# Two VectorE passes instead of three for each converted weight, range checks moved into the MLPs, and a new written-out order

## The chip, the core and the metric

The kernel runs on one core of one Trainium2 chip. The metric is the device time of one execution in microseconds; the median of three executions of the kernel before is 641.96 us (640.41 to 643.04).

## The reference, cut to what matters

A linear recurrence runs over 768 steps for 4 x 8 heads of dimension 40, and its output goes through an MLP without a nonlinearity other than one product:

```python
for t in range(S):                                  # S = 768
    y[:, :, t] = einsum('bhd,bhde->bhe', r_t, state)
    Sa = einsum('bhde,bhe->bhd', state, a_t)
    state = state * w_t[:, :, None, :] - einsum('bhd,bhe->bhde', Sa, b_t)
    state = state + einsum('bhd,bhe->bhde', v_t, k_t)
x = y.transpose(0, 2, 1, 3).reshape(3072, 320)
h = ((x @ w1) * (x @ w2)) @ w3                      # w1, w2: 320 x 1024, w3: 1024 x 1024
out = (h @ w_out).astype(float32)                   # w_out: 1024 x 320
```

The weights arrive as 64-bit floats. The kernel reads them as 64-bit integers and makes 32-bit floats of them on the chip.

## The kernel before, in words

The 768 steps are cut into 12 chunks of 64 (`NCH`), and the 32 heads into two groups (`NG`). For a chunk and group the kernel loads a block `fm` (decays and two operands) and a block `lh` through SyncE's queue (`load`), makes running products of the decays on VectorE and scales the operands with them on VectorE or GpSimd (`scale`, L397 to L422), and forms the products inside a chunk on TensorE (`causal`, L446). For a chunk, `solve` inverts the triangular matrices that couple its steps: a transpose into PSUM (tile `ab`, L478), some 40 short VectorE operations (L504 to L527) and two transposes (L554, L557), the results of which stand in `TDX`. For the first three chunks `merge` (L582 to L594) does a part of this on TensorE, between a first and a second L557. `join` (L618, L625) builds the joined inverse in `TT`, with four ScalarE copies `TT<-TDX` at its end. `pairs` (L662) and `tokens` (L689) prepare operands. `rec` is the recurrence proper: for a group TensorE does L713, L720, L728 and L744 one after the other, with ScalarE copies and GpSimd masks between them, and L779 carries the state on; it depends on the chunk before. `gather` (L801) moves the chunk's output `y` into the MLP's layout `xr` by twelve DMAs, and `mlp` does the MLP of a chunk: 128 matrix products with `W12` (L843) and 48 with `W3` (L869), 16 and 7 us of TensorE.

`W3` stands for w3 @ w_out, which is multiplied out once (`product`, L365). An MLP needs `W12`, that is w1 and w2, in a high and a low part: a ScalarE copy makes the high part and a GpSimd subtraction (L343, L355) the low one.

`weights` and `convert` make the 32-bit weights, in 16 pieces of up to 128 x 1024 (15.5 pieces' worth, 1 MB each): a DMA into `raw` (two buffers), on ScalarE a square (L291) and an exponential (L294), each with a sum that serves a range check, and on VectorE three passes: L297 with one input, L301 and L304 with two. The order of pieces is: one row block of w1 and w2, then w_out, then w3 with the products, then the rest of w1 and w2. The sums are judged at the very end of the program text (L1016 to L1027), in instructions that do not belong to the written-out order: the judging of the weights' sums (L1019) was put where its inputs were ready, between two passes of the last piece. The verdict decides whether a slow general path runs; in these executions it does not.

Nothing is scheduled at run time. Each engine runs its instructions in the order in which they were written, and `PLAN`, a packed table of numbers, sets that order for all of them (`Order.place`), together with the buffer that each tile takes. `SLOTS` says how many buffers a tile has.

Of the kernel before, what the change touches and what calls it, by code (L numbers as in the profile page):

```python
# [1096 lines left out]
```

## Time and profile before

| | before |
|---|---|
| median of 3 executions | 641.96 us |
| the profiled execution | 644.88 us |
| its span, first to last instruction | 643.2 us |
| mean granted TensorE clock | 0.974 |
| TensorE (PE) busy | 575.1 us, 89% |
| VectorE (DVE) busy | 464.4 us, 72% |
| ScalarE (ACT) busy | 465.6 us, 72% |
| GpSimd (POOL) busy | 243.7 us, 38% |
| DMA moved | 57.65 MB, 90 GB/s |

Busy times are summed over each engine's instructions; a share says nothing yet on where an engine waits. The span is 1.68 us shorter than the execution's own time, and that execution was 2.92 us longer than the median.

### The profile page before, as it was taken

To read this page: it belongs to the slowest core of one execution; us is meant where nothing else is said; L and a number is where in the kernel's file an instruction comes from. 1 tells how busy PE (TensorE), PEld (TensorE's weight loads), DVE (VectorE), ACT (ScalarE), POOL (GpSimd) and SP (SyncE) were. 2 spreads that over 40 slices of the span, in tenths; PEclk is the share of its full clock that TensorE was granted. 3 is DMA by queue.
4 is the path that set the end of the run, shared out by engine and by line. 5 is a ranking of instruction groups with operands and counts; after the bars stand their busy time and mean duration, and the time that the engine had idled before them with its cause. 6 is when DMAs were issued, how large, how long until landed. Compare 5 with 4: busy or idle time off the path is not lost.

```text
span 643.2 us, 23611 instructions
## 1 busy us (share of the span) xinstructions
PE 575.1 (89%) x10226; PEld 521.6 (81%) x10226; DVE 464.4 (72%) x795; ACT 465.6 (72%) x962; POOL 243.7 (38%) x229
## 2 busy tenths in 40 slices
PE   0534989969999999899999999999999999999996
PEld 0424666649899999899999989998898999999995
DVE  7997989795469789369789695897796875931320
ACT  1785778888866977777977878778777689676321
POOL 5152075143551315542426336236254165321011
PEclk9999998976999999899999999999998999999998
DMA  8755466433314314314243144143340341211101
GB/s 191 220 142 200 147 217 170 121 94 89 73 33 93 87 43 93 83 48 107 59 98 93 37 99 85 46 99 78 82 112 20 88 110 33 63 26 29 32 21 25
DMA packets 58935, 57.65 MB, mean 90 GB/s; under 512 B 29320, under 2 KB 52360, under 8 KB 56904
## 3 DMA queue, kind: packets, MB, share of 16 engines
q1 hardware_dynamic: 58824, 56.07, 34.4%
q8 instruction: 82, 1.34, 0.9%
q14 instruction: 29, 0.24, 0.1%
HBM read 47.40 MB, written 3.93 MB: 80 GB/s over the span
## 4 chain that ended last, share of the span: by engine, by line
PE 62%; DVE 16%; DMA 9%; ACT 6%; issue 4%; POOL 1%; SPq 1%; DVEq 0%; POOLq 0%; ACTq 0%
PE bank L843 21%; PE bank L869 12%; DMA fm<-in_fmx_dram 6%; PE bank L365 4%; PE bank L720 4%; PE bank L744 4%; PE bank L446 3%; PE bank L728 2%; PE bank L713 2%; DVE tmp L504 2%; PE bank L689 2%; PE bank L779 2%; PE bank L618 2%; PE bank L625 2%; DVE mf L301 2%
## 5 line engine op out<-in xcount | busy, mean ns | idle before, releaser
L843 PE MATMUL bank<-xs,W 128*128 128x256 f32 x1536 | 204.9, 286 | 1.6 <-issue 1.5
L843 PEld LDWEIGHTS bank<-xs,W 128*128 128x128 f32 x1536 | 187.7, 189 | 8.1 <-issue 2.0
L177 ACT ACTIVATE xu<-bank 64x416 f32<-64x416 f32 (+2 forms) x280 | 123.8, 462 | 34.8 <-PE bank L728 16.6
L737 POOL TENSOR_SCALAR_AFFINE_SELECT xu<-xu 64x512 f32<-64x512 f32 x48 | 37.1, 773 | 152.8 <-ACT xu L177 136.2
L860 POOL TENSOR_TENSOR gl<-ga,gh 128x512 fp32r<-128x512 f32 x32 | 44.2, 1384 | 74.6 <-ACT gh L177 74.5
L177 ACT ACTIVATE JP<-bank 32x512 f32<-32x512 f32 (+1 forms) x120 | 59.8, 500 | 17.3 <-PE bank L446 9.8
L857 DVE TENSOR_TENSOR ga<-bank,ga 128x512 f32<-128x512 f32 x48 | 32.7, 684 | 49.9 <-PE bank L843 20.7
L464 POOL TENSOR_SCALAR_AFFINE_SELECT lh<-lh 64x512 f32<-64x512 f32 x48 | 38.6, 808 | 66.4 <-ACT lh L177 65.0
L869 PE MATMUL bank<-W3h,gh 128*128 128x320 f32 x192 | 63.7, 332 | 0.0
L869 PE MATMUL bank<-W3l,gh 128*128 128x320 f32 x192 | 60.5, 315 | 0.0
L869 PE MATMUL bank<-W3h,gl 128*128 128x320 f32 x192 | 60.5, 315 | 0.0
L672 POOL TENSOR_SCALAR_AFFINE_SELECT xu<-xu 64x512 f32<-64x512 f32 x48 | 39.6, 828 | 27.2 <-ACT xu L177 25.4
L177 ACT ACTIVATE gh<-ga 128x512 fp32r<-128x512 f32 x48 | 30.0, 628 | 22.7 <-DVE ga L857 22.0
L177 ACT ACTIVATE ga<-bank 128x512 f32<-128x512 f32 x48 | 28.5, 594 | 24.1 <-PE bank L843 21.5
L744 PE MATMUL bank<-xu,bk 128*40 128x104 f32 (+1 forms) x768 | 41.1, 260 | 5.4 <-POOL xu L737 5.3
L720 PE MATMUL bank<-xu,lh 104*64 104x104 f32 (+2 forms) x768 | 44.1, 267 | 1.9 <-ACT xu L177 0.9
L422 POOL TENSOR_TENSOR fm<-fm,gi 104x1024 f32<-104x1024 f32 x12 | 31.3, 2611 | 38.1 <-DMA rv<-in_rv_dram 13.7
L397 DVE TENSOR_TENSOR_SCAN fm<-fm,first 104x520 f32<-104x520 f32 x24 | 31.6, 1317 | 17.8 <-DMA fm<-in_fmx_dram 17.7
L409 POOL TENSOR_TENSOR lh<-lh,fm 104x1024 f32<-104x1024 f32 x16 | 35.3, 2208 | 21.5 <-DVE fm L397 18.8
L720 PEld LDWEIGHTS bank<-xu,lh 104*64 104x64 f32 (+2 forms) x768 | 38.0, 144 | 6.5 <-issue 1.9
L744 PEld LDWEIGHTS bank<-xu,bk 128*40 128x40 f32 (+1 forms) x768 | 35.4, 121 | 9.5 <-POOL xu L737 7.2
L478 DVE STREAM_TRANSPOSE ab<-JP 128x1024 f32<-128x1024 f32 x12 | 24.0, 2004 | 26.0 <-ACT JP L177 26.0
(104 smaller groups left out, 1189.9 us busy)
## 6 DMA issues: line engine op xcount, KB each, us to landing
fm<-in_fmx_dram SPq DMA_DIRECT2D x24, 627.2 KB
raw<-in_w3t_dram SPq DMA_DIRECT2D x8, 1024.0 KB
rv<-in_rv_dram SPq DMA_DIRECT2D x48, 160.0 KB
raw<-in_w_dram SPq DMA_DIRECT2D x4, 1024.0 KB
lh<-in_fma_dram SPq DMA_DIRECT2D x48, 80.0 KB
xu<-in_vt_dram SPq DMA_DIRECT2D x48, 80.0 KB
out_dram<-o SPq DMA_DIRECT2D x48, 80.0 KB
xr<-y SPq DMA_DIRECT2D x72, 40.0 KB
```

The source lines that it names most:

```text
L177: act.activation(out_, in_, AF.Copy, scale=scale)
L397: dve.tensor_tensor_scan(out=w, data0=w, data1=first.rearrange("p n t -> p (n t)"), initial=0.0, op0=ALU.mult, op1=ALU.max)
L409: e.tensor_tensor(out=lh.t[0:104], in0=lh.t[0:104], in1=gam(c, g)[:, :, 0:C].unsqueeze(1).to_broadcast(full), op=ALU.mult)
L464: pool.affine_select(out=lh.t[q, ab], in_=lh.t[q, ab], pattern=[[0, NP], [1, C]], compare_op=ALU.is_gt, fill=0.0, base=0, channel_multipli ...
L672: op("pool", 0.67, due + 2, lambda q=q, ab=ab: pool.affine_select(out=xu.t[q, ab, :, 0:C], in_=xu.t[q, ab, :, 0:C], pattern=[[0, NP], [1, ...
L720: pe.matmul(out=view(hp[h])[64 * ab:64 * ab + 64, u], lhsT=lh.t[k, ab, HP * h + u], rhs=xu.t[k, ab, HP * h + u], start=True, stop=True)
L737: pool.affine_select(out=u, in_=u, pattern=[[0, NP], [1, C]], compare_op=ALU.is_gt, fill=0.0, base=0, channel_multiplier=-1)
L744: pe.matmul(out=q(r, p), lhsT=bk.t[:, p, r], rhs=xu.t[:, ab, p], start=(c == 0), stop=True, skip_group_check=True)
L843: pe.matmul(out=pt.t[:, TOK * x:TOK * x + TOK], lhsT=WT[k][:, cs], rhs=xs.t[:, z], start=(n == 0), stop=(n == 7))
L857: op("dve", 0.69, t, lambda a=a, pt=pt: dve.tensor_tensor(out=a.t, in0=wide(pt), in1=a.t, op=ALU.mult), r=[pt], w=[a])
L860: both(ON["gl"][c % NCH], 1.3, 0.69, t + 1, lambda e, a=a, j=j: e.tensor_tensor(out=gl.t[:, j:j + 2], in0=a.t, in1=gh.t[:, j:j + 2], op=AL ...
L869: pe.matmul(out=pt.t[:, 0:DM], lhsT=l.t[:, j, ts], rhs=W3[r][:, j], start=(j == 0 and n == 0), stop=(j == NJ - 1 and n == 2))
```

## The change

A piece of weights is now converted in two VectorE passes of two inputs each. What the third pass did (bringing in bits of the low word) is prepared by one ScalarE copy of 16-bit numbers into a new tile `low`, which has one buffer. `raw` has three buffers instead of two. Pieces of w1 and w2 are converted in halves of 512 columns (`KW`), and so are their ScalarE copies and GpSimd subtractions. w_out and w3 come first now, and all of w1 and w2 after them.

The range checks no longer use what `convert` has loaded. 31 pieces of 512 columns are read from memory anew, from the first MLP on, into a tile `ck` with one buffer: a DMA of 512 KB, a ScalarE square with a sum, and a VectorE minimum. Their judging is now part of the written-out order (`verdict`), before the program's end.

`solve` writes the transposed inverse straight into the right half of `TT`, which has two buffers now, so that `join` copies two blocks instead of four. `fm` and `lh` have five buffers instead of four. The table `PLAN` is new: the work is ordered anew throughout.

```diff
-SLOTS = dict(rc=1, fm=4, lh=4, ..., JP=2, TT=1, bank=6, raw=2, sq=1, mf=2, w3f=2, ...)
+SLOTS = dict(rc=1, fm=5, lh=5, ..., JP=2, TT=2, bank=6, raw=3, ck=1, low=1, mf=2, w3f=2, ...)
 PLAN = """
-c-oa%3Ak0ok*?}<?%PywnGiBAnM{@u1H>ebVTeKy1F|bf6crRSfFL^>hA1fN7!}zBmDL!7h!6o~Q4usIG11THr_LBM!OR$u;7o#ovOL~9UGrCU-*eA>IL<
+c-nPX378edwLVqdmzfb<kQhZ-1R;DVE`(K)C4d_yfDi;R(SQatfk2{091t842%;i_AjngORb>~WL=gcIf}?_9Kt)7@s2@-LU}Tx)R-N~ss_wph!8iAtzJ0
...
-ON = dict(ws="p", ...)
+ON = dict(ws="ppppp", ...)
 def convert(src, dst, due, w=(), n=CW):
-    raw, sq, mf = slot("raw"), slot("sq"), slot("mf")
+    raw, low = slot("raw"), slot("low")
+    sources.extend(src[:, f:min(f + KW, n)] for f in range(0, n, KW))
+    parts = [slot("mf") for _ in range(0, n, KW)] if dst is None else [None]
     def f2():
-        act.activation(sq.t[:, 0:n], raw.t.bitcast(BF16)[:, 3:4 * n:4], AF.Square, accum_out=wstats[:, k:k + 1])
+        act.activation(low.t.bitcast(U16)[:, 0:2 * n:2], raw.t.bitcast(U16)[:, 1:4 * n:4], AF.Copy, scale=7.49 / 65535.0)
-    def f3():
-        act.activation(sq.t[:, 0:n], sq.t[:, 0:n], AF.Exp, scale=-2.0 ** 23, accum_out=wstats[:, NCV + k:NCV + k + 1])
-    def f4():
-        dve.tensor_scalar(out=M(), in0=H(), scalar1=3, scalar2=0xC0000001, op0=ALU.logical_shift_left, op1=ALU.bitwise_or)
-    def f5():
-        dve.scalar_tensor_tensor(out=M(), in0=H(), scalar=0x3FFFFFFF, in1=M(), op0=ALU.bitwise_or, op1=ALU.bitwise_and)
-    def f6():
-        dve.scalar_tensor_tensor(out=M() if dst is None else dst().bitcast(U32), in0=L(), scalar=29, in1=M(), ...)
+    def f3(i, M):
+        dve.scalar_tensor_tensor(out=M(), in0=H(a, b), scalar=3, in1=low.t[:, a:b], op0=ALU.logical_shift_left, op1=ALU.bitwise_or)
+    def f4(i, M):
+        dve.scalar_tensor_tensor(out=M(), in0=H(a, b), scalar=0x3FFFFFFF, in1=M(), op0=ALU.bitwise_or, op1=ALU.bitwise_and)
+def ranges(k, due):
+    raw, n = slot("ck"), sources[k].shape[-1]
+    B = lambda: raw.t.bitcast(BF16)[:, 3:4 * n:4]
+    def f1():
+        sp.dma_start(out=raw.t[:, 0:n], in_=sources[k])
+    def f2():
+        act.activation(B(), B(), AF.Square, accum_out=wstats[:, k:k + 1])
+    def f3():
+        dve.tensor_reduce(out=wstats[:, NCV + k:NCV + k + 1], in_=B(), axis=mybir.AxisListType.X, op=ALU.min)
+    op("sp", 0.351, due - 8, f1, r=["W12"], w=[raw, "turn"], dma=5.0 * n / 1024)
...
 def solve(c, due, span):
-        TD = tdx.t[:, 0:512].rearrange("x (p t) -> x p t", t=32)
+        TD = tt.t[:, :, 32:64]
-        dve.transpose(out=tdx.t[:, 512:1024], in_=tdx.t[:, 0:512])
+        dve.transpose(out=tdx.t.rearrange("x (p t) -> x p t", t=32), in_=tt.t[:, :, 32:64])
 def join(c, due):
-    for q in range(4):
-        op("act", 0.65, due + 5, lambda r=r, q=q: copy(tt.t[r, :, 32 * (q % 2):32 * (q % 2) + 32], half(0)[r]), ...)
+    for b in range(2):
+        op("act", 0.65, due + 2, lambda r=r: copy(tt.t[r, :, 0:32], tt.t[r, :, 32:64]), r=[(tt, "e", b)], w=[(tt, "c", b)])
```

**VectorE at the first chunk's merge.** Of the kernel before, from the first chunk's transpose to the sum that ends its merge (L594); TensorE's merge products stand between the two. A name's number tells one tile from the next; `w3f` and `wof` are converted weights.

```order
L557 STREAM_TRANSPOSE TDX_99<-TDX_99 128x512
L304 SCALAR_TENSOR_TENSOR wof<-raw_138,mf_141 128x512
L297 TENSOR_SCALAR mf_141<-raw_139 128x1024
L301 SCALAR_TENSOR_TENSOR mf_141<-raw_139,mf_141 128x1024
L304 SCALAR_TENSOR_TENSOR w3f_147<-raw_139,mf_141 128x1024
L594 TENSOR_TENSOR TDX_99<-bank_132,TDX_99 128x16x16
```

Of the change, the same stretch, whose transpose stands two rows above (L298 and L302 are the two passes, L412 to L433 belong to `scale`, L612 is the sum that was L594):

```order
L302 SCALAR_TENSOR_TENSOR w3f_155<-raw_144,w3f_155 128x1024
L412 SCALAR_TENSOR_TENSOR fm_93<-fm_93,first 104x520
L493 STREAM_TRANSPOSE ab<-JP_113 128x1024
L519 TENSOR_TENSOR tmp<-DG,ab 128x4
L523 TENSOR_REDUCE DG<-tmp 128x4
L519 TENSOR_TENSOR tmp<-DG,ab 128x16
L298 SCALAR_TENSOR_TENSOR w3f_154<-raw_145,low_146 128x1024
L302 SCALAR_TENSOR_TENSOR w3f_154<-raw_145,w3f_154 128x1024
L428 SCALAR_TENSOR_TENSOR gt_100,stats<-fm_93,gi_99 104x512
L433 SCALAR_TENSOR_TENSOR gi_99<-gt_100,gi_99 104x512
L523 TENSOR_REDUCE DG<-tmp 128x4x2
L612 TENSOR_TENSOR TT_114<-bank_136,TT_114 128x16x16
```

Before, four operations stand between the transpose and the sum; now twelve do, four passes and the next chunk's transpose (L493) among them.

**VectorE at the last piece of w1 and w2.** Of the kernel before (L772 is the state of `rec`):

```order
L297 TENSOR_SCALAR mf_141<-raw_139 128x1024
L301 SCALAR_TENSOR_TENSOR mf_141<-raw_139,mf_141 128x1024
L1019 TENSOR_SCALAR stats<-stats 128x16
L304 SCALAR_TENSOR_TENSOR mf_141<-raw_139,mf_141 128x1024
L772 TENSOR_TENSOR st_107<-bank_129,fm_92 104x160
```

Of the change:

```order
L519 TENSOR_TENSOR tmp<-DG,ab 128x144
L298 SCALAR_TENSOR_TENSOR mf_147<-raw_143,low_146 128x512
L302 SCALAR_TENSOR_TENSOR mf_147<-raw_143,mf_147 128x512
L298 SCALAR_TENSOR_TENSOR mf_148<-raw_143,low_146 128x512
L302 SCALAR_TENSOR_TENSOR mf_148<-raw_143,mf_148 128x512
L523 TENSOR_REDUCE DG<-tmp 128x4x6
```

The judging (L1019) is gone from this place, and the last piece runs in two halves.

**TensorE ahead of the first MLP.** Of the kernel before, the rows that stand 20 to 16 rows ahead of the first product of an MLP (L843); L582 and L588 are the third chunk's merge, L720 and L728 the second group's recurrence of the second chunk:

```order
L582 MATMUL bank_129<-TDX_99,JP_110 32x16 x64
L720 MATMUL bank_134<-xu_102,lh_95 64x104 x8
L720 MATMUL bank_132<-xu_102,lh_95 64x104 x8
L588 MATMUL bank_129<-TDX_99,wa 32x16 x64
L728 MATMUL bank_132<-hs_106,TT_112 64x104
```

Of the change, the second five of the first MLP's rows (L857, which was L843), and what follows them, the second group's recurrence (L734, which was L720):

```order
L857 MATMUL bank_135<-xs_1539,W_0_86 128x256 x2
L857 MATMUL bank_135<-xs_1539,W_2_87 128x256
L857 MATMUL bank_135<-xs_1539,W_1_1356 128x256 x2
L857 MATMUL bank_135<-xs_1539,W_3_1357 128x256
L857 MATMUL bank_135<-xs_1539,W_4_1358 128x256 x2
L734 MATMUL bank_136<-xu_105,lh_98 64x104 x8
L734 MATMUL bank_138<-xu_105,lh_98 64x104 x8
```

The third chunk's merge and the second group's L720 and L728 now stand behind the first MLP's first products instead of ahead of them.

## Rows read from the trace of the kernel before

**Rows 1.** Busy time by stretch: length, PE, PEld, DVE, ACT, POOL, PEclk, DMA share, GB/s.

```profile
17.00:64.00 47.00, 21.99 (x601) 18.62 (x601) 41.60 (x60) 35.07 (x74) 15.76 (x12) 1.00 0.64 185
64.00:143.10 79.10, 70.00 (x1175) 51.43 (x1175) 69.07 (x110) 63.41 (x123) 31.83 (x22) 0.93 0.51 154
143.10:157.20 14.10, 12.97 (x401) 11.58 (x401) 8.06 (x16) 11.27 (x24) 4.75 (x2) 0.57 0.29 73
157.20:636.60 479.40, 469.97 (x8054) 439.81 (x8050) 332.65 (x598) 352.66 (x736) 182.15 (x172) 0.99 0.29 67
```

**Rows 2.** Timeline of TensorE ahead of the first MLP: start, length, engine, what.

```profile
156.32 0.94 PE L728 MATMUL bank<-hs,TT 64*64 64x104 f32 x32
157.19 2.99 PE L843 MATMUL bank<-xs,W 128*128 128x256 f32 x23
```

**Rows 3.** Timeline of VectorE from the last piece to the first MLP.

```profile
139.47 2.55 DVE L1019 TENSOR_SCALAR stats<-stats 128x16 f32<-128x16 f32 x1 [0.36 <-ACT sq L291]
141.93 1.21 DVE L304 SCALAR_TENSOR_TENSOR mf<-raw,mf 128x1024 uint32<-128x1024 uint32 x1
...
150.50 1.91 DVE L397 TENSOR_TENSOR_SCAN fm<-fm,first 104x520 f32<-104x520 f32 x1 [2.85 <-DMA fm<-in_fmx_dram]
153.17 0.96 DVE L829 TENSOR_TENSOR xs<-xr,xs 128x768 fp32r<-128x768 f32 x1 [0.77 <-ACT xs L826]
```

**Rows 4.** Instructions that read `raw`: duration ns minimum/median/maximum, first and last start.

```profile
L297 DVE TENSOR_SCALAR mf<-raw x16: 419/686/1345, 24.1 to 136.8; 128x1024 uint32<-128x1024 uint32 x15, 128x512 uint32<-128x512 uint32 x1
L301 DVE SCALAR_TENSOR_TENSOR mf<-raw,mf x16: 668/1224/3269, 25.8 to 137.5; 128x1024 uint32<-128x1024 uint32 x15, 128x512 uint32<-128x512 uint32 x1
```

**Rows 5.** Groups by line and shape: busy us, mean ns, idle before and its releasers.

```profile
L297 DVE TENSOR_SCALAR mf<-raw 128x1024 uint32<-128x1024 uint32 x15 | 11.8, 789 | 2.3 <-DMA raw<-in_w3t_dram 1.6 <-POOL W L343 0.6
L294 ACT ACTIVATE sq<-sq 128x1024 f32<-128x1024 f32 x15 | 15.8, 1053 | 0.3
```

**Rows 6.** Timeline of VectorE's memsets at the start.

```profile
5.39 0.91 DVE L225 MEMSET SB<- 104x1024 f32 x1 [0.16 <-issue]
```

**Rows 7.** What VectorE waited for from 7 to 157.2 us: total, times, longest.

```profile
DVE TDX L594 <- PE bank L588: 7.4, 3, 3.9
DVE fm L397 <- DMA fm<-in_fmx_dram: 3.4, 2, 2.9
...
DVE mf L297 <- DMA raw<-in_w3t_dram: 1.6, 1, 1.6
```

**Rows 8.** Timeline of VectorE and GpSimd near 30 us.

```profile
30.00 3.27 DVE L301 SCALAR_TENSOR_TENSOR mf<-raw,mf 128x1024 uint32<-128x1024 uint32 x1
29.44 2.75 POOL L422 TENSOR_TENSOR fm<-fm,gi 104x1024 f32<-104x1024 f32 x1 [13.68 <-DMA rv<-in_rv_dram]
```

**Rows 9.** Timeline of TensorE between 116 and 186 us.

```profile
116.16 0.72 PE L588 MATMUL bank<-TDX,wa 32*32 32x16 f32 x64
117.90 0.73 PE L588 MATMUL bank<-TDX,wa 32*32 32x16 f32 x64
177.79 1.65 PE L720 MATMUL bank<-xu,lh 128*64 128x104 f32 x32
184.83 0.94 PE L728 MATMUL bank<-hs,TT 64*64 64x104 f32 x32
```

**Rows 10.** Groups by line and shape, of work that is nearest to the new.

```profile
L291 ACT ACTIVATE sq<-raw 128x512 f32<-128x512 bf16 x1 | 0.7, 666 | 0.0
L291 ACT ACTIVATION_READ_ACCUMULATOR sq<-raw 128x1 f32 x16 | 3.1, 194 | 0.0
L508 DVE TENSOR_REDUCE Tp<-tmp 128x64 f32<-128x512 f32 x18 | 12.3, 683 | 0.4
L177 ACT ACTIVATE TT<-TDX 32x512 f32<-32x512 f32 x48 | 30.1, 627 | 2.9 <-DVE TDX L594 1.9 <-DVE TDX L554 0.2
```

**Rows 11.** What SyncE's queue waited for in the whole execution, its longest.

```profile
SPq L385 <- DVE y L791: 59.2, 9, 10.3
```

More of the change, by code (lines that the diff above doesn't have):

```diff
@@ new lines, in convert @@
+        op("sp", 0.35, due - 8, f1, w=[raw, "turn"], dma=5.0 * n / CW)
+        op("act", 0.21 + 0.852 * n / CW, due, f2, r=[raw], w=[low])
+        for i, mf in enumerate(parts):
+            M = (lambda mf=mf: mf.t) if mf else lambda: dst().bitcast(U32)
+            to = [mf] if mf else w
+            op("dve", 0.17 + 1.071 * step / CW, due, lambda i=i, M=M: f3(i, M), r=[raw, low], w=to, two=True)
+            op("dve", 0.17 + 1.071 * step / CW, due, lambda i=i, M=M: f4(i, M), r=[raw, "conv"], w=to, two=True)
@@ L330, in weights @@
+        for ib in range(NJ):
+            w3f = slot("w3f")
+            convert(w3t[ib], lambda w3f=w3f: w3f.t, due, w=[w3f])
+            due += step
+            product(ib, w3f, due)
+        op("nil", 0.0, due, second, w=["reg2"])
+        for k in range(3):
             for f in range(2048 // CW if k < 2 else DFF // CW):
-                cs = slice(CW * f, CW * f + CW)
-                due = split(k, f, cs, due)
-                due += step
-        op("nil", 0.0, due, third, r=[("W", k, f) for k in range(3) for f in range(2)], w=["W12", "conv"])
+                due = split(k, f, slice(CW * f, CW * f + CW), due) + step
@@ L336, in split @@
+        op("nil", 0.0, due, third, r=[("W", k, f, i) for k in range(3) for f in range(2) for i in range(2)], w=["W12", "conv"])
     def split(k, f, cs, due):
         over = ["conv"] if k == 0 else ["conv", "reg2"]
-        if k < 2:
-            mf = convert(w12[k * 128:k * 128 + 128, cs], None, due)
-            def f2(e):
-                e.tensor_tensor(out=WT[2 + k][:, cs], in0=mf.t.bitcast(F32), in1=WT[k][:, cs], op=ALU.subtract)
-            op("act", 1.06, due, lambda: copy(WT[k][:, cs], mf.t.bitcast(F32)), r=[mf, *over], w=[("W", k, f)])
-            both(ON["ws"], 2.45, 1.22, due, f2, r=[mf, *over], w=[("W", k, f)])
-            return due
@@ L348, in split @@
[L348 to L356 removed]
+        parts = convert(w12[k * 128:k * 128 + 128, cs] if k < 2 else w12c[:, cs], None, due)
@@ L629, in blocks @@
             return t[r].rearrange("x (p t) -> x p t", t=32)
[L631 to L632 removed]
+        op("pe", 1.1, due, f1, r=[tdx, *[(jp, g, 2 * i) for g in range(NG) for i in range(2)]], w=[p1], kind="32")
         for b in range(2):
```

255 lines of the change are left out of this document (130 added, 125 removed).

## The prediction

> **What bounds the kernel now.** I first cut the span into stretches, because the shares of the whole (PE 89%, DVE and ACT 72%) mix two quite different stages [rows 1]. From 157.2 us, where the first MLP's products begin, to the last product TensorE is busy 469.97 of 479.40 us at a granted clock of 0.99: there TensorE is the bound, and all that can be had is the 9.4 us in which it idles. Ahead of it the picture is the reverse. From 17 to 64 us TensorE is busy 22 of 47 us, from 64 to 143 us 70 of 79 us with part of it at a lower clock (mean 0.93), and from 143 to 157 us the granted clock is 0.57, near the lower of its two levels, 1.2 GHz. VectorE in the same stretches is busy 41.6 of 47 and 69.1 of 79 us. So the kernel has a first stage of 157 us that VectorE sets, and a second that TensorE sets. TensorE's work after the first MLP's start is the same whatever happens before. So the question is when the first MLP starts, and how much of TensorE's work is left then.
>
> Second, what holds that start: the timeline of VectorE ahead of it [rows 3]. The last pass over the last piece (L304) starts at 141.93 us, behind the judging L1019, which waits 0.36 us and takes 2.55 us for 16 columns. Then VectorE waits 2.85 us for a load of `fm`, and makes the MLP's low input (L829) from 153.17 to 154.13 us. TensorE takes the MLP up at 157.19 us, as it is still in the work that stands ahead in its order [rows 2].
>
> **The change part by part, as a sum for the MLP's start.**
>
> Conversion: a piece of 1024 columns costs medians of 0.69 us for the one-input pass and 1.22 us for each two-input pass, a half 0.67 us [rows 4]. Before: 15.5 pieces x (0.69 + 1.22 + 1.22) = 48.5 us. After: 10.5 pieces of w_out and w3 x 2 x 1.22 = 25.6 us, and 5 pieces of w1 and w2 x 4 halves' passes x 0.67 = 13.4 us, together 39.0 us. Term: -9.5 us; at most -12.2 us, if the removed passes are taken as they ran (11.8 us for 15, [rows 5], and 0.42 us for the half).
>
> These rows show that the removed pass was the cheapest: it ran at almost twice the others' rate. The Trainium skill states why (VectorE: DVE Perf Modes, section "Mode 2×_2P — use both read ports for one tensor"): an operation with one tensor input may use both read ports, one with two inputs can't. Its table of costs (section "The TRN2 errata") would give, as an estimate, (58 + 512) / 0.96 GHz = 0.59 us for the removed pass and 0.06 us more for every extra half, so 15.5 x 0.59 - 10 x 0.06 = 8.6 us instead of 9.5.
>
> Encounters with GpSimd: a pass that began at 30.00 us beside a GpSimd product (29.44 to 32.19 us) took 3.27 us [rows 8], so that the encounter cost 2.05 us over the median. There were 48 passes and are 42 (22 for w_out and w3, 20 halves for w1 and w2), and the subtractions that they can meet are as many columns as before. I count this at nothing, with 6 x 2.05 = 12 us to gain at most and 5 x 2.05 = 10 us to lose, if each of the five pieces of w1 and w2 has one encounter more, as four short passes are met more easily than three long ones.
>
> The skill has the rule for this (SBUF — State Buffer, section "SBUF: two separate sides"): VectorE and GpSimd share a port pair, and whoever comes second waits for the whole instruction. The row agrees, and by the rule a reduction with one input, which each new check is, does not wait at all (section "Who interferes with whom").
>
> Judging: L1019 and its wait leave the path, -2.9 us [rows 3]. The new judging stands near the program's end, where VectorE has time.
>
> Memsets: a fifth `lh` and a second `TT`, 2 x (0.91 + 0.16) = +2.1 us at the start [rows 6]. They stand ahead of the first scan. At worst they are hidden by nothing, and that is what I take.
>
> The first merge: VectorE waited 3.9 us for TensorE there [rows 7], with four operations between. Now four passes (4 x 1.22 us), the next chunk's transpose, a scan and more stand there. Term -3.9 us; 0 if TensorE, which has a product of w3 in front of its merge and one between the merge's halves, is later by as much.
>
> Loads: VectorE waited 1.6 us for `raw` and 2.9 us of 3.4 us for `fm` ahead of the MLP [rows 7]. A third `raw` and a fifth `fm` let these loads go out earlier. I take half, -2.3 us, between 0 and -4.5.
>
> New wait: the first pass now needs ScalarE's copy into `low`, which has one buffer, and behind a late copy ScalarE's in-order queue holds the copies of the recurrence. The nearest rows are the square and the exponential of the same piece, 1.05 us for the latter [rows 5], and these held up nobody but the judging. Bounds: 0, as the two old ScalarE operations were twice as long and no pass waited for them, and 15.5 x 1.05 = 16.3 us if every copy is on the path. I take +2 us, near the lower end, since ScalarE was busy 63 of 79 us in the stage and loses over a us per piece.
>
> TensorE's lateness at the MLP: 3.1 us between L829's end and the first product [rows 2, 3]. The rows of the order show what stood in front, the third chunk's merge and the second chunk's second recurrence group, behind the MLP's first products now. I take -2 us of it.
>
> Sum: -9.5 - 2.9 + 2.1 - 3.9 - 2.3 + 2 - 2 = -16.5 us, that is a first MLP at 140.7 us instead of 157.2.
>
> Against it stands what is only put off. The merge's two halves (twice 1.45 us; L582 is counted like L588), L720 with 1.65 and L728 with 0.94 us [rows 9] now come after the MLP's start, 5.5 us; smaller differences in the order ahead of it (fewer transposes, one `causal` more) add up to half a us. So +6.0 us.
>
> Second stage: the 31 checks add a reduction of 0.68 us each to VectorE (21 us) and a square with its sum's reading, 0.67 + 0.19 us, to ScalarE (27 us), while the shorter join takes 24 copies of 0.63 us away (15 us in all) [rows 10]. That makes VectorE busy some 74% of this stage instead of 69, ScalarE about 76 instead of 74 [rows 1]. TensorE covers this as it does now; not covered, it is rival two. The loads add 31 x 0.52 = 16 MB, some 40 GB/s on 67 if they spread over 400 us. I take 0, between -9.4 us (TensorE's idle time gone, with five buffers for `fm` and `lh`) and +21 us.
>
> The end: the last product still comes last, with the same 128 and 48 products of the last MLP behind the same amount of the one before. 0.
>
> Net: -16.5 + 6.0 = -10.5 us. The sum is made against the profiled execution, 644.88 us (span 643.2): 634.4 us; it lay 2.92 us above the median, so as a median 631.5 us.
>
> **The rivals.**
>
> One, more than that: SyncE's queue waited 59 us, in nine waits, for a free `fm` [rows 11], and some of TensorE's idle time goes back to late loads. If the fifth buffers end them and 7 of 9.4 us go as well: 624.5 us. Against it: TensorE idles only 2% there, spread over short waits.
>
> Two, the checks cost TensorE time and the kernel gets slower. Each of the 31 stands in front of work of the recurrence on VectorE and ScalarE, and its load stands in SyncE's queue in front of `rv`, `fm` and `xr` loads, where it must wait until the one before is read, as `ck` has one buffer. Behind a late `rv` waits L713, behind a late `fm` the scan. If each delays the recurrence, and TensorE runs out of products, by its 0.68 us: +21 us, 652.5 us. It turns the sign when 16 of 31 do (10.5 / 0.68). For it: the two engines are at three quarters already. Against it: the MLP's products are there as filler, and TensorE hardly idled beside engines almost as busy.
>
> Three, the conversion does not come sooner: the loads of the first stage ran at 185 and then 154 GB/s [rows 1], and 15.5 MB of weights with `fm` and the rest have to come in 140.7 us instead of 157.2, some 12% faster than that; or every pass waits for ScalarE's copy. Then only the judging and TensorE's lateness are saved: -2.9 + 2.1 - 2 + 6.0 = +3.2 us, about 645 us. Against it: the DMA share was 0.64 and 0.51 there.
>
> **How the numbers follow.** The forecast (626 to 638 us by its own terms) has 0.50, rival one 0.20, rival two 0.15, rival three 0.15. What a measurement of this kernel can tell from no change is 0.5%, 3.2 us: 638.8 to 645.2 us count as the same. Faster: 0.49 of the forecast, 0.20, and 0.02 each of two and three where they hold in part, 0.73. Same: 0.01, 0.04 of two, 0.09 of three, 0.14. Slower: 0.09 of two and 0.04 of three, 0.13. The predicted time is 631.5 us. For 8 in 10 the range leaves out the last of rival two (652.5 us) and the best of rival one: 619 to 647 us.
>
> **What would show it.** Right: the first MLP's products at 135 to 146 us; the two passes' lines at about 39 us plus encounters; the merge's wait on TensorE under 2 us; no wait of the passes on ScalarE over a few us; TensorE idle for 5 to 15 us from there to its end. Wrong: VectorE's first pass waiting long for `low` or `raw`, a first MLP after 150 us (rival three), or TensorE idle for 20 us and more behind VectorE, ScalarE or late loads in the second stage (rival two).

## The result, and the profile after

The change makes the kernel slower: a median of 648.03 us (644.98 to 650.75, 8 runs) against 640.85 us (639.31 to 643.04, 8 runs) of the kernel before on the same chip, a ratio of 1.0112 [1.0085, 1.0139]. The profiled execution took 647.18 us (span 645.5).

The first view to read is again busy time by stretch, with the columns and the first stretches of [rows 1]:

```profile
17.00:64.00 47.00, 29.18 (x578) 22.68 (x575) 41.21 (x59) 29.75 (x59) 12.27 (x9) 0.89 0.70 212
64.00:143.10 79.10, 61.82 (x1212) 45.90 (x1200) 64.62 (x104) 55.36 (x100) 43.74 (x32) 0.89 0.49 146
143.10:157.20 14.10, 12.98 (x176) 11.54 (x177) 9.50 (x19) 11.96 (x23) 5.76 (x7) 0.88 0.51 132
157.20:256.00 98.80, 90.56 (x1773) 84.07 (x1772) 74.48 (x138) 77.90 (x164) 30.44 (x30) 0.95 0.46 122
157.20:636.60 479.40, 465.89 (x8234) 436.01 (x8233) 337.35 (x627) 373.17 (x774) 171.41 (x169) 0.99 0.37 98
```

From 157.2 us on ScalarE has 20 us more to do than before, and the DMAs move 98 GB/s instead of 67. TensorE is idle for 13.5 us of this stretch instead of 9.4, and 8.2 of the 13.5 lie in its first 99 us, where its granted clock is 0.95 too.

**When the first MLP starts.** The timeline of TensorE, which answers to [rows 2] (L857 was L843):

```profile
148.36 0.54 PE L793 MATMUL bank<-ident,st 104*40 104x104 f32 x4
148.74 0.35 PE L857 MATMUL bank<-xs,W 128*128 128x256 f32 x1
```

It starts at 148.74 us instead of 157.19, and the forecast was 140.7. What VectorE waited for up to 157.2 us, as in [rows 7]:

```profile
DVE mf L298 <- POOL W L359: 7.2, 1, 7.2
DVE gt L428 <- ACT gi L419: 4.3, 3, 1.6
DVE w3f L298 <- ACT low L294: 3.6, 2, 3.4
DVE W3l L385 <- ACT W3h L180: 2.6, 1, 2.6
...
DVE TT L612 <- PE bank L606: 1.3, 1, 1.3
DVE fm L412 <- DMA fm<-in_fmx_dram: 1.2, 1, 1.2
...
DVE mf L298 <- ACT low L294: 0.5, 2, 0.3
```

The merge's wait (1.3 us), the wait for `fm` (1.2 us) and that for `raw` (none) are small, as forecast. At the head stands a wait that the prediction does not have. Timelines of VectorE, GpSimd, ScalarE and TensorE around it (in brackets the idle time before an instruction, and what ended it):

```profile
127.86 2.07 DVE L298 SCALAR_TENSOR_TENSOR mf<-raw,low 128x512 uint32<-128x512 uint32 x2 [7.16 <-POOL W L359]
```
```profile
125.83 2.50 POOL L359 TENSOR_TENSOR W<-mf,W 128x512 fp32r<-128x512 f32 x2 [6.60 <-ACT W L180]
```
```profile
125.05 1.15 ACT L180 ACTIVATE W<-mf 128x512 fp32r<-128x512 f32 x2 [0.69 <-PE bank L380]
```
```profile
117.05 0.45 PE L461 MATMUL bank<-lh,fm 40*64 40x64 f32 x12 [3.06 <-issue]
117.43 4.11 PE L380 MATMUL bank<-wof,w3f 128*128 128x320 f32 x8
121.47 1.20 PE L636 MATMUL bank<-TDX,JP 32*32 32x32 f32 x64
122.60 2.42 PE L380 MATMUL bank<-wof,w3f 128*128 128x320 f32 x8
```

Read from below: the last w3 products (L380) are late, at a granted clock of 0.58 (117.4 to 121.5 us) behind a stall of 3.06 us. ScalarE may copy a piece of the second row block of w1 and w2 into `W` only when they are done, since `wof` and `w3f` have that memory (`reg2`). GpSimd subtracts behind the copy, and VectorE needs the `mf` that both still read. There are two `mf` as before, but each holds 512 columns now instead of 1024: one piece ahead instead of two.

The two passes themselves, the groups that answer to [rows 4, 5], and the copy that feeds them:

```profile
L294 ACT ACTIVATE low<-raw 128x1024 uint16<-128x1024 uint16 x15 | 20.4, 1360 | 5.7 <-DVE w3f L298 5.6
L298 DVE SCALAR_TENSOR_TENSOR w3f<-raw,low 128x1024 uint32<-128x1024 uint32 x8 | 10.9, 1366 | 3.6 <-ACT low L294 3.6
L302 DVE SCALAR_TENSOR_TENSOR w3f<-raw,w3f 128x1024 uint32<-128x1024 uint32 x8 | 10.1, 1265 | 0.2
L298 DVE SCALAR_TENSOR_TENSOR mf<-raw,low 128x512 uint32<-128x512 uint32 x10 | 8.8, 907 | 7.7 <-POOL W L359 7.2 <-ACT low L294 0.5
L302 DVE SCALAR_TENSOR_TENSOR mf<-raw,mf 128x512 uint32<-128x512 uint32 x10 | 8.2, 841 | 0.1
```

**Behind the first MLP.** What TensorE waited for from 148 us to the end, its longest, and the timeline of the place (`issue` is time in which the engine waited for nothing that the profile shows):

```profile
PE bank L606 <- issue: 5.0, 1, 5.0
PE bank L461 <- issue: 2.8, 3, 1.1
PE bank L643 <- issue: 0.9, 1, 0.9
```
```profile
162.11 1.16 PE L676 MATMUL bank<-rv 40*64 40x64 f32 x64
163.20 1.26 PE L600 MATMUL bank<-TDX,JP 32*32 32x16 f32 x128
164.44 0.30 PE L461 MATMUL bank<-lh,fm 40*64 40x64 f32 x2
165.10 0.44 PE L461 MATMUL bank<-lh,fm 40*64 40x64 f32 x10 [0.36 <-ACT xu L180]
166.60 1.03 PE L461 MATMUL bank<-lh,fm 40*64 40x64 f32 x52 [1.07 <-issue]
167.57 1.03 PE L606 MATMUL bank<-TT,wa 32*32 32x16 f32 x76
173.62 0.93 PE L606 MATMUL bank<-TT,wa 32*32 32x16 f32 x52 [5.03 <-issue]
174.48 0.95 PE L703 MATMUL bank<-ident,fm 104*128 104x104 f32 x4
175.13 3.76 PE L857 MATMUL bank<-xs,W 128*128 128x256 f32 x16
```

TensorE stops in the middle of the third chunk's merge (L600 and L606, which were L582 and L588), with 76 of 128 products of L606 done, and waits for nothing that the trace knows. The 16 products of L857 behind it take 0.235 us each, twice as long as in the 58 that the kernel before had there (7.10 us, behind a stall of 1.53 us). The granted clock shows it, in the stretches from 168 to 176 and from 176 to 184 us of the changed kernel:

```profile
170.76 7.10 PE L843 MATMUL bank<-xs,W 128*128 128x256 f32 x58 [1.53 <-issue]
```
```profile
168.00:176.00 8.00, 2.97 (x105) 2.82 (x95) 1.14 (x2) 2.46 (x6) 2.35 (x3) 0.54 0.76 178
176.00:184.00 8.00, 8.00 (x114) 7.75 (x113) 5.07 (x11) 5.26 (x10) 1.30 (x2) 0.82 0.01 2
```

What it waits for is its instructions. They come in packets of 16,384 bytes on a DMA queue of their own; the profile's page has 82 of them (`q8 instruction: 82, 1.34`). One began at 171.1 us and took 1.14 us, and TensorE went on 1.4 us later; the stalls at 166.60 and 117.05 us ended 1.4 and 1.5 us behind such a packet too. The count agrees: from the end of one stall to the next TensorE ran the 52 products of L461 and the 76 of L606, each with its weight load, 256 instructions. The packet at 171.1 us began 4.4 us after TensorE had begun those 256, the latest of 80 in this profile (median 0.7 us, worked out from the trace's packets and instructions). In the eight microseconds of the stall the data's DMAs were busy 0.76 of the time, for an `fm`, a `ck` and smaller transfers issued together. The Trainium skill has the first half of that (Runtime: NRT & Kernel Launch, section "Instruction fetch mechanics"): an engine's instructions stream in, in blocks of 16 KiB that hold 256 of them, over a queue that its sequencer drives, and it calls the cost mostly hidden. The packets and the count agree; that it is hidden does not hold here.

**The checks.** Groups of the square (L323) and the minimum (L326), to be set beside [rows 10]:

```profile
L323 ACT ACTIVATE ck<-ck 128x512 bf16<-128x512 bf16 x31 | 42.3, 1365 | 0.2
L326 DVE TENSOR_REDUCE stats<-ck 128x1 f32<-128x512 bf16 x31 | 21.1, 682 | 16.7 <-ACT ck L323 16.4
L323 ACT ACTIVATION_READ_ACCUMULATOR ck<-ck 128x1 f32 x31 | 8.2, 265 | 0.0
```

The minimum costs the 0.68 us that I took; the square 1.365 us instead of 0.67 and its sum's reading 0.265 instead of 0.19, 50 us of ScalarE instead of 27. VectorE stood 16.4 us behind squares.

**Where the time is.** A ledger of TensorE from each profile, worked out from stretches of 2 us: when its first MLP product starts; from there on its work (busy time times granted clock), its idle time, and what it lost to the lower clock; then what lies between its last product and the span's end. The last four rows are kernels of the next section ("dense" is a square written side by side, "filled" a merge with long products in it).

| profile | MLP start | work | idle | clock | tail |
|---|---|---|---|---|---|
| before, two profiles | 157.2, 155.2 | 466.2, 466.2 | 10.0, 7.6 | 3.4, 1.7 | 6.4, 6.3 |
| after, four (means) | 148.4 | 470.4 | 13.85 | 4.9 | 7.2 |
| after, difference of means | -7.8 | +4.2 | +5.05 | +2.4 | +0.85 |
| forecast | -16.5 | +6.0 | 0 (with the clock) | | 0 |
| no checks, third comparison | 149.1 | 468.3 | 7.3 | 2.5 | 6.5 |
| dense squares, fourth | 148.5 | 468.3 | 9.3 | 2.6 | 7.2 |
| dense squares, filled merge | 147.6 | 468.5 | 4.0 | 1.8 | 7.2 |
| no checks, filled merge | 148.0 | 468.3 | 6.4 | 3.4 | 6.6 |

The MLP starts 7.8 us sooner and the rest costs 12.5 us, which makes +4.7 us of the profiles; by the medians at the head of this section it is 7.2. Against the four profiles with checks, the one without them has 6.6 us less idle time, 2.4 less lost to the clock, 2.1 less work and 0.7 less tail: that is how the checks reach TensorE.

### The profile page after: what moved, and what is told of

It reads as the page before. It is cut to its first block, busy times and chain, and to the rows that moved or that the text cites. A ratio compares the mean times of both kernels' runs of the same rounds, so it can differ in the third digit from the quotient of the medians.

```text
span 645.5 us, 23738 instructions
## 1 busy us (share of the span) xinstructions
PE 572.8 (89%) x10226; PEld 518.8 (80%) x10226; DVE 465.7 (72%) x822; ACT 473.6 (73%) x959; POOL 241.0 (37%) x236
## 3 DMA queue, kind: packets, MB, share of 16 engines
q8 instruction: 82, 1.34, 0.9%
## 4 chain that ended last, share of the span: by engine, by line
PE 62%; DVE 15%; ACT 10%; issue 5%; DMA 4%; POOL 1%; SPq 1%; DVEq 0%; ACTq 0%; POOLq 0%
PE bank L857 24%; PE bank L883 11%; PE bank L758 4%; PE bank L734 4%; PE bank L380 3%; DMA fm<-in_fmx_dram 3%; ACT xu L180 3%; PE bank L742 2%; PE bank L461 2%; PE bank L793 2%; PE bank L703 2%; ACT ck L323 2%; PE bank L727 2%; PE bank L643 2%; DVE tmp L519 2%
## 5 line engine op out<-in xcount | busy, mean ns | idle before, releaser
L857 PE MATMUL bank<-xs,W 128*128 128x256 f32 x1536 | 203.6, 288 | 1.7 <-DVE xs L843 0.6
L857 PEld LDWEIGHTS bank<-xs,W 128*128 128x128 f32 x1536 | 189.3, 192 | 6.0 <-DVE xs L843 1.0
L874 POOL TENSOR_TENSOR gl<-ga,gh 128x512 fp32r<-128x512 f32 x32 | 42.2, 1322 | 79.9 <-ACT gh L180 77.8
L461 PE MATMUL bank<-lh,fm 40*64 40x64 f32 x1536 | 33.6, 239 | 37.8 <-DVE fm L437 15.7
L461 PEld LDWEIGHTS bank<-lh,fm 40*64 40x64 f32 x1536 | 29.9, 151 | 41.4 <-issue 30.2
L883 PE MATMUL bank<-W3h,gh 128*128 128x320 f32 x192 | 62.5, 325 | 0.3 <-ACT lh L180 0.3
L883 PE MATMUL bank<-W3l,gh 128*128 128x320 f32 x192 | 59.3, 309 | 0.0
L883 PE MATMUL bank<-W3h,gl 128*128 128x320 f32 x192 | 59.2, 308 | 0.0
L380 PE MATMUL bank<-wof,w3f 128*128 128x320 f32 x128 | 44.4, 503 | 3.6 <-ACT low L294 3.2
L479 POOL TENSOR_SCALAR_AFFINE_SELECT lh<-lh 64x512 f32<-64x512 f32 x48 | 36.6, 765 | 28.0 <-ACT lh L180 26.8
L437 POOL TENSOR_TENSOR fm<-fm,gi 104x1024 f32<-104x1024 f32 x12 | 29.4, 2453 | 46.7 <-DVE DG L523 22.4
L424 POOL TENSOR_TENSOR lh<-lh,fm 104x1024 f32<-104x1024 f32 x16 | 35.1, 2195 | 29.8 <-DVE fm L412 23.6
L734 PE MATMUL bank<-xu,lh 104*64 104x104 f32 (+2 forms) x768 | 42.9, 265 | 0.7 <-ACT xu L180 0.6
L323 ACT ACTIVATE ck<-ck 128x512 bf16<-128x512 bf16 x31 | 42.3, 1365 | 0.2
```

The lines of the kernel that those rows point to most:

```text
L323: act.activation(B(), B(), AF.Square, accum_out=wstats[:, k:k + 1])
L380: pe.matmul(out=pt.t[:, 0:DM], lhsT=w[:, j], rhs=wof[:, j], start=(j == 0), stop=(j == NJ - 1))
L461: pe.matmul(out=bank(ab)[64 * x:64 * x + 64, p], lhsT=X[r, p, x], rhs=lh.t[r, ab, p], start=True, stop=True)
L479: pool.affine_select(out=lh.t[q, ab], in_=lh.t[q, ab], pattern=[[0, NP], [1, C]], compare_op=ALU.is_gt, fill=0.0, base=0, channel_multipli ...
L734: pe.matmul(out=view(hp[h])[64 * ab:64 * ab + 64, u], lhsT=lh.t[k, ab, HP * h + u], rhs=xu.t[k, ab, HP * h + u], start=True, stop=True)
L857: pe.matmul(out=pt.t[:, TOK * x:TOK * x + TOK], lhsT=WT[k][:, cs], rhs=xs.t[:, z], start=(n == 0), stop=(n == 7))
```

## The experiments

Ratios are to the kernel before in the same comparison, with the 95% interval. Before's medians were 643.47, 645.09, 643.20, 642.70 and 643.65 us in the five.

**First: which part of a check costs.** Without the checks:

```diff
-            sp.dma_start(out=raw.t[:, 0:n], in_=sources[k])
+            pass
-            act.activation(B(), B(), AF.Square, accum_out=wstats[:, k:k + 1])
+            pass
-            dve.tensor_reduce(out=wstats[:, NCV + k:NCV + k + 1], in_=B(), ...)
+            pass
```

> The changed kernel without the 31 range checks: their loads, squares and minima are left out, and the sums that the verdict reads are set once. All else stands in the same order. Theory A (the checks cost TensorE time, rival two): the time falls by 5 us or more, to 643 us or below (ratio to the kernel before under 1.004), and the stall of 5.03 us inside L606 at 168.6 us is gone. Theory B (the checks are hidden, and the first stage alone gave too little): 646 to 649 us, ratio 1.008 to 1.013, with the same stall.

638.24 us, 0.9889 [0.9837, 0.9941]. The checks are what turns the sign. The stall inside L606 (L607 in this kernel) is not gone, but 1.3 us.

Without their loads alone (the first pair of lines):

> The changed kernel with the checks' squares and minima, but without their 31 loads (they read a tile that is set once). If the loads are what costs (they fill the DMA engines just when TensorE's own instructions must be fetched, 16 KB at a time): as fast as without the checks. If the engines' time is what costs (a square takes 1.36 us and not the 0.67 us that I took): no faster than the changed kernel, 648 us. If the checks cost nothing: 646 to 649 us for this one and for the one without checks.

643.95 us, 1.0013 [0.9979, 1.0046]: back to the time before, not faster.

The loads alone (the other two pairs):

> The changed kernel with the checks' 31 loads, without their squares and minima. If the loads cost: 646 to 649 us as the changed kernel. If ScalarE's and VectorE's time costs: as fast as without the checks. A part that both share shows in both as half of the gain.

640.81 us, 0.9972 [0.9941, 1.0004]: slower than without checks, and faster than the changed kernel's 1.0112. So the loads and the engines' part both cost something. The changed kernel itself was not in this comparison.

The square, written side by side instead of into its own places 8 bytes apart:

```diff
+        Q = lambda: raw.t.bitcast(BF16)[:, 0:n]
-            act.activation(B(), B(), AF.Square, accum_out=wstats[:, k:k + 1])
+            act.activation(Q(), B(), AF.Square, accum_out=wstats[:, k:k + 1])
-            dve.tensor_reduce(..., in_=B(), axis=mybir.AxisListType.X, op=ALU.min)
+            dve.tensor_reduce(..., in_=Q(), axis=mybir.AxisListType.X, op=ALU.min)
```

> The changed kernel with the squares of the checks written side by side (2 bytes apart) into the front of the same tile instead of back to their places 8 bytes apart; nothing is left out. If the spread of the output sets the price of a square: 0.67 us each instead of 1.36 us, 21 us less of ScalarE's busy time, and VectorE's minimum the same or shorter. In the time: theory A with ScalarE as the cause gains a third to all of what the kernel without checks gains; theory B, and theory A with the loads as the cause, gain under 1 us.

641.33 us, 0.9979 [0.9945, 1.0013]. The groups of its square and minimum:

```profile
L324 ACT ACTIVATE ck<-ck 128x512 bf16<-128x512 bf16 x31 | 20.7, 667 | 0.2
L327 DVE TENSOR_REDUCE stats<-ck 128x1 f32<-128x512 bf16 x31 | 21.0, 677 | 8.7 <-ACT ck L324 8.7
L324 ACT ACTIVATION_READ_ACCUMULATOR ck<-ck 128x1 f32 x31 | 5.9, 191 | 0.0
```

The same square, read from the same places, takes half as long when only its output lies side by side. The expectation's "a third to all" came true: of the fall from 1.0112 to 0.9889 without checks, this kernel has more than half. VectorE's wait behind squares falls from 16.4 to 8.7 us.

**Second: later checks, and more `mf`.** My next theory was that checks cost because they stand where the second stage is tight, and that the first stage is held by `mf`. The moves of these and the next kernels are pairs in the table that sets the order: take an operation out and put it in front of another.

```diff
+        for n, before in MOVES:
+            turns.remove(n)
+            turns.insert(turns.index(before), n)
```

All checks' operations moved to some 420 us and later, the square dense, three buffers for `ck` (two of them memory that is free by then):

> The changed kernel with dense squares, and with all 31 checks moved behind 430 us: 15 of them between 430 and 550 us, 16 behind 556 us, where little of the recurrence is left and VectorE is busy a third of the time (these in three buffers, two of them tiles that are no longer used). Theory A' (a check costs where it stands in front of the recurrence's copies and loads, and nothing where TensorE has the products of an MLP before it): ratio to before 0.987 to 0.992, as without the checks, and no long stall in L606. Rival (the 16 MB and 27 us of ScalarE cost the same wherever they stand): 0.996 to 1.000, as with dense squares alone.

661.35 us, 1.0252 [1.0209, 1.0296]. That theory falls, and its rival too: these late checks cost more than the early ones. What TensorE, ScalarE and VectorE waited for from 400 or 430 us on, their rows that concern the checks and the recurrence (L736, L795 and L802), and two stretches:

```profile
PE bank L802 <- DVE st L795: 5.6, 2, 5.0
PE bank L736 <- ACT TT L187: 2.7, 1, 2.7
```
```profile
ACT ck L332 <- DMA ck<-in_w3t_dram: 9.8, 4, 6.1
```
```profile
DVE stats L335 <- ACT ck L332: 15.1, 8, 4.2
```
```profile
528.00:538.00 10.00, 8.68 (x129) 8.45 (x130) 3.36 (x3) 7.92 (x17) 0.00 (x0) 0.66 0.38 101
560.00:572.00 12.00, 9.13 (x101) 8.52 (x102) 6.39 (x12) 6.19 (x14) 2.58 (x3) 0.57 0.46 141
```

A square waits for its load, a minimum for its square, the recurrence's state (L795) stands behind them on VectorE, and TensorE runs dry and loses clock.

Four `mf` and two `raw` (`raw=2, ..., mf=4` in `SLOTS`), the last two pieces' operations moved up, the square dense; and the same with the late checks:

> Dense squares, checks where they were; four buffers of 512 columns for mf instead of two (paid for with the third raw), and the last two pieces' ScalarE copies, VectorE passes and GpSimd subtractions moved up some ten places in the order each. Theory C (what held the first MLP is the round trip VectorE, ScalarE, GpSimd through mf, of which the change had left buffers for one piece only): VectorE's wait of 7 to 8 us for mf at 120 us is gone or under 2 us, and the first MLP's products start 3 to 8 us sooner than with dense squares alone (149.1 us). Rival (the round trip only takes up slack; the recurrence of the first chunk or TensorE's products of w3 hold the MLP): it starts within 2 us of 149. The time: 1 to 3 us less by theory C, as TensorE's own idle time there is what counts.

> Both edits together: dense squares, all checks behind 430 us, and four buffers for mf with the last pieces moved up. If theories A' and C hold and add up: ratio to the kernel before 0.980 to 0.988, the best so far; if only the checks' place counts, as that kernel alone.

648.02 us, 1.0059 [1.0021, 1.0097], and 665.32 us, 1.0299 [1.0244, 1.0354]. In the first the wait for `mf` behind GpSimd is gone and the last copy into `W` starts at 139.7 us instead of 145.3, but the first MLP starts at 155.17 us (in the second at 154.23): neither what theory C nor what its rival expected. Timelines of TensorE and VectorE ahead of it:

```profile
141.54 0.61 PE L742 MATMUL bank<-xu,lh 128*64 128x104 f32 x2 [4.56 <-ACT xu L187]
...
155.17 2.13 PE L865 MATMUL bank<-xs,W 128*128 128x256 f32 x16
```
```profile
152.57 0.33 DVE L794 TENSOR_TENSOR st<-bank,fm 104x160 f32<-104x160 f32 x1 [5.71 <-PE bank L766]
```

The copies into `W` now stand in front of the copies of the first chunk's recurrence on ScalarE, and the MLP waits for that instead. The passes also wait more for `low` there, 7.9 us (in the second 5.4) instead of 4.1. So `mf` was a hold, but not the only one, and what more `mf` would bring in an order made for it isn't shown.

The changed kernel in the same comparison:

> The changed kernel once more, on the same chip as the three below, to compare them with it. All theories: a ratio to the kernel before of 1.008 to 1.014. In its profile TensorE again waits 3 to 6 us for instructions inside L606 at about 170 us, as the stretch ahead of it is the same; a wait under 2 us there would say that it was chance.

648.02 us, 1.0039 [1.0007, 1.0071]: slower again, by less than expected. Its stall in L606 is 4.1 us, as expected.

**Third: the checks' price.**

> The changed kernel on the same chip as the kernel without checks and as the kernel before, to price the checks within one comparison. All theories: ratio to the kernel before 1.003 to 1.014.

> The changed kernel without the 31 checks (loads, squares and minima left out) again. Theory A: 8 to 14 us below the changed kernel of the same comparison, ratio to the kernel before 0.985 to 0.994. Theory B: within 2 us of it.

> The kernel before against itself, for a second profile of it: a ratio of 0.997 to 1.003, which says what these comparisons can tell apart; TensorE's idle time behind 157 us 8 to 11 us as in the first profile (9.4), or less, as the first profiled execution was 3 to 4 us above the median.

648.97 us, 1.0124 [1.0070, 1.0178]; 636.61 us, 0.9924 [0.9896, 0.9952]; 642.47 us, 1.0001 [0.9965, 1.0037]. The checks cost 648.97 - 636.61 = 12.4 us, 0.40 us each, as theory A has it.

The checks dense, and spread from 186 us on, one in 11.5 us:

> The changed kernel with dense squares, and the checks spread evenly from 186 us on, one in 11.5 us: none beside the merge at 170 us, each square some 7 us behind its load and each minimum some 3 us behind its square in the order, so that no engine has to wait for a check. Nothing is left out. Theory A'' (of the checks' price the waits and the starved TensorE at 170 us are the larger part, the work itself the smaller): half or more of what the kernel without checks gains, ratio to before 0.990 to 0.995, TensorE's idle time behind 157 us 8 to 10 us instead of 13.5. Rival (16 MB and the engines' time cost by themselves): 0.996 to 1.003.

647.38 us, 1.0075 [1.0038, 1.0112]: a miss of both. VectorE's waits behind squares fell to 2.4 us, but TensorE idled 11.6 us and lost clock at other places. That VectorE waits for squares is then not by itself the price.

**Fourth: dense, without loads, and a filled merge.** In the last of these 16 long products of the first MLP, the GpSimd operation that belongs to them and the third check's load are moved between the merge's first and second half:

```diff
+MOVES = ((311, 655), (582, 655), (312, 655), (313, 655))
```

with the dense square and its minimum as above.

> The changed kernel on the same chip as the three below, so that the parts of the checks' price can be read within one comparison: 1.004 to 1.013 of the kernel before.

> Dense squares alone again. If the spread output of the squares makes half or more of the checks' price of about 12 us: 6 us or more below the changed kernel of this comparison. If it is ScalarE's time in proportion (24 of 50 us of it saved, with the loads' part as it was): 3 to 5 us below. If it is nothing, the first comparison of it was chance between chips: within 2 us.

> The checks' squares and minima without their loads again: 2 to 6 us below the changed kernel, if the loads have a price of their own (the first comparison gave loads alone 2.6 us over no checks); within 2 us if not.

> Dense squares, with the third check's load behind the loads of fm, lh and xu of 165 to 173 us instead of between them, and with 16 products of the first MLP moved from behind the merge's second half (L606) to ahead of it; nothing left out. Theory D (the merge that the change puts off behind the first MLP's start costs 5 to 6 us of idle TensorE and 4 to 5 us of its clock, as 192 short products use up the fetched instructions while the next 16 KB wait behind the loads): TensorE's wait in L606 falls from 4 to 5 us to under 2.5 us, and the time by 2 to 6 us against dense squares alone. Rival (the fetch comes when it comes, and filling only moves the wait): the wait stays at 4 us or comes elsewhere, and the time within 2 us.

647.87 us, 1.0108 [1.0052, 1.0165]; 639.87 us, 0.9971 [0.9937, 1.0006]; 644.38 us, 1.0053 [1.0018, 1.0089]; 632.29 us, 0.9871 [0.9816, 0.9925]. Dense squares give back 8.0 us, a figure clear of noise, and the absence of the loads 3.5, which the two intervals do not tell from nothing. That the loads cost something rests on the first comparison, where the loads alone had 0.9972 against 0.9889 without checks. The 12.4 us is from another comparison, so these parts need not add up to it. The filled merge with the dense square is 7.6 us faster again than the dense square alone, and beats both kernels: 10.4 us under before, 15.6 under the change. TensorE's timeline in it:

```profile
166.17 2.15 PE L863 MATMUL bank<-xs,W 128*128 128x256 f32 x16
168.26 0.69 PE L612 MATMUL bank<-TT,wa 32*32 32x16 f32 x60
170.04 0.76 PE L612 MATMUL bank<-TT,wa 32*32 32x16 f32 x68 [1.09 <-issue]
```

The stall is 1.09 us where the dense square alone still had 5.5, and the granted clock is 0.79 from 168 to 176 us and 1.00 from 176 to 184.

The profiles also settle what the third check's load does to this stall. Where it stands beside the merge, in the changed kernel, with dense squares, with four `mf` or with the loads alone, the stall is 3.7 to 5.5 us in eight profiles; without loads, without checks or with the checks moved away it is 1.3 to 2.9 us in six. The packet that TensorE waits for begins 4.4 us after the 256 instructions before it in the changed kernel's first profile, 1.5 and 1.2 us after them in the two without checks.

**Fifth: the fill by itself**, the same moves without the load's and without the dense square, **and with no checks**:

> The changed kernel with nothing but the 16 products of the first MLP ahead of the merge's second half (L606); squares in place, the third check's load where it was. Theory D (the put-off merge's starved wait by itself costs 6 to 8 us): 640 to 643 us, ratio to the kernel before 0.995 to 1.003, and a wait in L606 of 1 to 3 us. Rival (the gain needed the third check's load out of the way): a wait of over 3 us and within 3 us of the changed kernel's 648.

> The changed kernel without the 31 checks (loads, squares and minima left out) and with the 16 products ahead of L606: both costs that the forecast had at nothing are taken away. If the forecast's other terms hold in sum: ratio to the kernel before 0.978 to 0.987 (the forecast was 10.5 us less, 0.984). If the shortfall of the first MLP's start (148.7 us instead of 140.7) counts in full: 0.990 or above.

645.44 us, 1.0070 [1.0031, 1.0108], a miss, though its stall fell to 2.0 us and its idle time to 9.3; and 633.52 us, 0.9839 [0.9794, 0.9884], inside the expected range. By itself the fill brings 2.4 to 3.5 us against the changed kernel's 647.87 to 648.97 of other comparisons, which the intervals do not tell from nothing; its profile is of the fastest of its twelve executions, 4.0 us under their median, and so shows it better than it is. The packet comes as late in it as in the changed kernel (4.6 us), and the long products cover part of that; with the load moved away it comes at 1.7 us. Why the fill brought 7.6 us together with the dense square and the moved load, and little alone, stays open.

## Why the prediction was wrong

**The step that failed** is "I take 0" for the second stage, between -9.4 and +21 us. Without the checks the kernel runs at 0.9924, with them at 1.0124. Rival two was right: the price is 0.40 us a check where it had 0.68, and 31 x 0.40 = 12.4 us is more than the 10.5 at which it turns the sign. Its mechanism was half right. The queue that it names did wait: SyncE's stood 54.8 us, in 15 waits, for a check's minimum before the next load of `ck`. TensorE's idle time did not come to the 20 us that were to show this rival, since parts of the price are clock and work. Of the two prices under it the reduction's held (0.682 us), the square's was taken from a row that has the same shape but another output: L291 of [rows 10] writes `sq` side by side, the checks write in place, 8 bytes apart, and that costs 1.365 us. That output alone accounts for 8.0 us of a price of some 12. The loads, which I let pass with "some 40 GB/s on 67", have a part of the rest: they hold up TensorE's instructions at the merge. "TensorE covers this" did not hold with VectorE busy 70% and ScalarE 78% of the stage: waits of some us left TensorE idle and, behind the longest, at a lower clock.

**The first MLP**, forecast at 140.7 us, came at 148.74. By terms:
- *Conversion*, -9.5: the medians held (1.22 us at 1024 columns, 0.69 at 512), and all groups of the passes fell from 57.6 to 44.7 us, 12.9 us and so more than the bound of 12.2, since the passes met GpSimd less. *Encounters*, 0: other lines took longer instead (L542 twice for over 2 us instead of 0.4); what VectorE's instructions took over their medians in the stage is 12 to 14 us before and 11 to 13 after, by two ways of grouping them. Right in sum, and with judging and memsets its busy time from 7 us to the MLP fell from 126.5 to 118.2 us.
- *Merge*, -3.9: its waits fell from 5.1 us in two to 1.3 in one. *Loads*, -2.3: -3.3 (1.6 and 2.9 us became 1.2). *Judging*, -2.9: gone from the path. *TensorE's lateness*, -2: better, its first product did not wait for all of L843. Right.
- *Wait for `low`*, +2: 4.1 us. The row that I took for the copy's cost, 1.05 us, was another format; the copy takes 1.36 us.
- Missing in the sum: the wait for `mf`, 7.2 us; the wait for `W3h` grew from 1.8 to 2.6 us. I read `mf=2` in `SLOTS` and that a piece has two halves, and did not put the two together. VectorE's idle time from 7 us to the MLP stayed at 23.6 us instead of falling by 4.6.
- What holds the start: the last pass, which the prediction took for it, ended at 140.1 us, only 3.0 us sooner than before. Behind it stand the copies into `W` on ScalarE and the subtractions on GpSimd, which end at 147.3 us, and then the MLP's low input (L843), which starts at 148.28 us.

**What is put off**, +6.0: +4.2 us of work, near enough, since the products with `W3` (L883, which was L869) also became a little shorter, 181.0 us in all instead of 184.7 and 182.4. But the merge, moved to 162 us, now stands among 384 short products in a row beside a burst of loads, and starves: 5.0, 4.1, 4.1 and 5.5 us in the four profiles. *The end*, 0: +0.85 us.

Rivals one and three did not occur. SyncE's waits for a free `fm` fell from 59.2 us [rows 11] to 13.4, but that ended no idle time of TensorE that can be seen; and the MLP did come sooner. The kernel without checks and with a filled merge runs at 0.984, what I forecast (631.5 / 641.96 = 0.984), but by other terms: the MLP at 148.0 instead of 140.7 us, paid back by less idle time and less work.

## What to carry to other kernels

A new operation takes its price from a row with the same access pattern of input and output, not only the same shape, and a tile made half as wide is half the buffer: count columns, not tiles. Where an engine works through hundreds of very short instructions, look for where its instructions come from and what loads go out at that moment, and put long work in between. An addition to an engine that is "only" three quarters busy was not hidden here: in in-order queues each one stands in front of something, and moving it later cost more.

## What the runs showed of the hardware

- A ScalarE square of 128x512 two-byte values takes 1.365 us with its output 8 bytes apart and 0.667 us with it side by side; reading its accumulator takes 0.265 us behind the one and 0.191 behind the other. The Trainium skill (SBUF — State Buffer, section "Door 1: The DMA port swizzle (why `[64,N]` ≈ `[32,N]`)") says that two accesses to a line of 16 bytes are enough for full rate, so that two-byte data may be strided freely up to eight elements. For the reads, four elements apart in both, the runs agree (a ScalarE copy of 128x512 that reads side by side takes 0.629 us, `gh<-ga`); for the writes they do not, and the measurement decides.
- TensorE stood still for up to 5.5 us behind a packet of its instructions; two stalls in a row lie exactly 256 of its instructions apart. A load of 512 KB beside it made the same stall 3.7 to 5.5 us instead of 1.3 to 2.9.
- With and behind such idle moments its granted clock was lower for some us: 0.54 and 0.82 in the two stretches of the stall of 5.03 us, 0.66 and 0.57 in those of the late checks, means between the two levels, 1.2 and 2.4 GHz. It was not so behind every one: from 17 to 44 us it was 1.00, with TensorE busy for 13.58 of the 27 us.
